# An adaLN block on one core: late modulation vectors as VectorE dot products, and a second full set of FFN weight buffers

## The chip, the cores and the metric

The kernel runs on one core of one Trainium2 chip. The metric is the device time of one execution in microseconds (us); the lower the better. Several executions are made of each kernel, and the median is given.

## The reference

The computation is one transformer block with adaptive layer norm. Six modulation vectors of 1024 values come from one row `c` by one product; everything else uses them.

```python
mod = (silu(c) @ w_mod).reshape(1, 6, 1, -1)        # w_mod: 1024 x 6144
sa, ca, ga, sb, cb, gb = (mod[:, i] for i in range(6))
h = layernorm(x) * (1 + ca) + sa                    # x: 2048 x 1024
q = h @ wq                                          # 1024 x 4096: 32 heads of 128
p = softmax(q @ k.T / sqrt(128))                    # the last 512 rows of the cache, 4 kv heads
x = x + ga * ((p @ v) @ wo)                         # wo: 4096 x 1024
h = layernorm(x) * (1 + cb) + sb
x = x + gb * ((silu(h @ w_gate) * (h @ w_up)) @ w_down)   # F = 3584
```

All inputs and the output are bf16.

## The kernel before

`fast_path` does the work; `general_path` stands behind a flag that `bound_final` (L983) computes, for scores too large for the plain exponential, and does not run here. TensorE's work is cut into four chunks (`cc`) of 512 rows.

**Startup.** Four tiles of x, the first two modulation vectors' weights (`wm`, L682), the weights of the first heads, K and V are loaded. The vectors `ca` and `sa` are computed as columns by TensorE, the first 512 rows are normalised and transposed, and the first three heads' q are made.

**The attention loop** (L1203 to L1215) has 128 steps, one head of one chunk each. Step k issues, in this order: a load of q weights in two of four steps, the scores and exponentials of head k (`emit_s`, L1025; the exponentials on ScalarE, L1034), the q projection of head k+3 (`emit_q`, L1015), then the tasks registered for step k, then the output product of head k-1 (`emit_o`, L1054). A task is a function and its arguments, registered with `at(step, function, ...)` (L806), and the tasks of one step run in the order in which they were registered. From step 13 on nearly every step has one `emit_wo` (L1090): eight matmuls of the output projection into one PSUM bank (`a_ps`), which VectorE then copies or adds into `acc` (L1102, L1104). Other tasks are loads of x and `wo`, transposes of the attention output by DMA (`xpose_o`, L1081), the layer norm of the next chunk and of the FFN's chunks (`plan_ln`), and the products `bound_wq` (L951, L955), 32 multiplications of weights with themselves on VectorE that feed the flag; four of them stand at step 32.

**The order.** In the attention loop DMAs and the statistics and bound products are pinned to the order in which the program issues them (`pin`, `fetch`); the scheduler of the framework places the rest by its own estimate. In the FFN the pins are off, and the scheduler decides the order of loads as well. Nearly all loads are issued by SP (SyncE), one after the other.

**Buffers.** Pools of equal buffers are handed out in turn, and a new tile waits until the old one in its buffer has been used: `hT` has 4 (8 KB per partition each), `blkA` 8, `blkB` 7, `blkC` 12. In PSUM four banks (tag "mm") are shared in turn by `q_ps`, `a_ps`, `o_ps` (three slots of a head's output in one bank) and `row_ps`; two pairs of banks hold scores, later the FFN's `gu_ps`. V lies in a tile of its own, `v_sb`, which is read last by the last output product of the attention loop.

**The late modulation vectors.** `ga` and `gb` (vectors 2 and 5) are needed as rows spread over all partitions (`ga_bc`, `gb_bc`, read at L1108 and L1192), `cb` and `sb` (4 and 3) as columns (`cb1`, `sb` in `modT`, read in the second layer norm at L856). They are computed during the first 33 steps in two pairs, (2, 4) and (5, 3). `load_rows` (L769) loads 1 MB of `w_mod` into a buffer of the `hT` pool. `mod_rows` (L774) runs 16 matmuls (L779) in which silu(c), repeated 32 times (`sil32`), is the weight and 512 columns of `w_mod` stream; four such products lie side by side in one bank. It runs in steps 5, 13, 21 and 29. VectorE copies the first half of the sum (L784) and adds the second (L788); the result goes to DRAM (`row_d`), and from there `load_gate` (L793) reads it back into all partitions and `load_cols` (L797) into columns, at steps 15 and 16 and again at 31 and 32. For `cb` VectorE then adds 1 (L802).

**The FFN loop** (L1217 ff.) goes over chunks; each has seven groups (`fg`) of four f-tiles. `load_gu` (L1154) loads a group's gate and up weights as four tiles of 512 KB, two of `wg` and two of `wu`, from the pool `blkB` of seven buffers. `emit_gu` (L1161) does eight matmuls with gate and eight with up weights for each f-tile (L1168); as long as tasks of the attention loop are left over (the last output projections among them), they run between the f-tiles. Then `emit_down` (L1181) multiplies with `w_down`.

Of the kernel before, what the change touches and what calls it, by code (L numbers as in the profile page):

```python
# [9 lines left out]
ALU = mybir.AluOpType  # L10
AX = mybir.AxisListType
BF16 = mybir.dt.bfloat16
FP32 = mybir.dt.float32
# [575 lines left out]
def fast_path(ctx, tc, flag, A_x, A_k_cache, A_v_cache, A_wq, A_wo, B_x, B_w_gate, B_w_up,  # L589
# [3 lines left out]
    nc = tc.nc  # L593
    P = 128
    _, S, D = A_x.shape
    _, Hkv, Sk, Dh = A_k_cache.shape
# [6 lines left out]
    TCW = 512  # L603
    NTC = S // TCW
    QT = TCW // P
    DT = D // P
# [5 lines left out]
    NFG = FT // 4  # L612
# [11 lines left out]
    wm_v = w_mod.rearrange("(dt p) n -> p dt n", p=P)  # L624
# [4 lines left out]
    const = ctx.enter_context(tc.tile_pool(name="const", bufs=1))  # L629
    xpool = ctx.enter_context(tc.tile_pool(name="xres", bufs=1))  # L630
    hpool = ctx.enter_context(tc.tile_pool(name="hT", bufs=4))
# [3 lines left out]
    wk = ctx.enter_context(tc.tile_pool(name="work", bufs=2))  # L635
    sm = ctx.enter_context(tc.tile_pool(name="small", bufs=4))
    psp = ctx.enter_context(tc.tile_pool(name="psum", bufs=4, space=bass.MemoryType.PSUM))
    dp = ctx.enter_context(tc.tile_pool(name="dram", bufs=4, space=bass.MemoryType.DRAM))
# [4 lines left out]
    def blkB(name, shape, dt=BF16):  # L643
        return pb_.tile(shape, dt, name=name, tag="B")

    def blkC(name, shape, dt=BF16):
        return pc_.tile(shape, dt, name=name, tag="C")

    def mm(name, shape=(P, 512), dt=FP32):
        return psp.tile(list(shape), dt, name=name, tag="mm", bufs=4)  # L650
# [9 lines left out]
    def pin(ins, what="steps"):  # L660
        return tc.keep_in_program_order(ins) if stage[what] else ins

    def fetch(out, in_):
        pin(nc.sync.dma_start(out=out, in_=in_), "dma")  # L664

    def load(out, in_):
        with nc.allow_non_contiguous_dma(reason="weight slice"):
            fetch(out=out, in_=in_)
# [33 lines left out]
    for kv in range(Hkv):  # L702
        pin(nc.sync.dma_start_transpose(
            out=kT[:, kv, :], in_=A_k_cache[0, kv, k0:k0 + W, :]), "dma")
    VN = Dh + 2
    v_sb = const.tile([P, Hkv, WT, Dh + 32], BF16, name="v_sb")
# [8 lines left out]
    ones_bf = const.tile([P, P], BF16, name="ones_bf")  # L715
# [15 lines left out]
    sa, ca1, sb, cb1 = (modT[:, i, :] for i in range(4))  # L731
    ga_bc = const.tile([P, D], FP32, name="ga_bc")
    gb_bc = const.tile([P, D], FP32, name="gb_bc")
# [7 lines left out]
    sil_r = const.tile([DT, P], BF16, name="sil_r")  # L741
# [3 lines left out]
    siluc = const.tile([P, DT], BF16, name="siluc")  # L745
# [12 lines left out]

    sil32 = const.tile([P, DT, 32], BF16, name="sil32")
    for dt in range(DT):
        nc.vector.tensor_scalar(out=sil32[:, dt, :], in0=ones_bf[:, 0:32],
                                scalar1=siluc[:, dt:dt + 1], scalar2=None, op0=ALU.mult)
    wm_rows = []
    row_part = []
    row_d = {}

    def load_rows(vec, part):  # L769
        t = hpool.tile([P, 4, D], BF16, name="wmr", tag="hT")  # L770
        load(t, wm_v[:, 4 * part:4 * part + 4, vec * D:(vec + 1) * D])
        wm_rows.append(t)

    def mod_rows(n, part):  # L774
        ps = mm("row_ps")
        tiles = [wm_rows.pop(0) for _ in range(2)]
        for k in range(4):
            for i in range(4):
                nc.tensor.matmul(ps[32 * i:32 * i + 32, :], lhsT=sil32[:, 4 * part + k, :],  # L779
                                 rhs=tiles[i // 2][:, k, (i % 2) * 512:(i % 2 + 1) * 512],  # L780
                                 start=(k == 0), stop=(k == 3))
        if part == 0:
            r = blkC("row", [P, TCW], FP32)
            nc.vector.tensor_copy(out=r, in_=ps)  # L784
            row_part.append(r)
        else:
            r = row_part.pop()
            nc.vector.tensor_tensor(out=r, in0=ps, in1=r, op=ALU.add)  # L788
            d = dp.tile([4, TCW], FP32, name="row_d", tag="row_d", bufs=2)
            fetch(out=d, in_=r[0:P:32, :])  # L790
            row_d[n] = d

    def load_gate(n, k, dst):  # L793
        fetch(out=dst.rearrange("p (a b) -> p a b", a=2),
                          in_=row_d[n][k:k + 2, :].partition_broadcast(P))

    def load_cols(n, k, dst, add_one):  # L797
        src = row_d[n][k:k + 2, :].rearrange("a (b p) -> p (a b)", p=P)
        with nc.allow_non_contiguous_dma(reason="1024 values to columns"):
            fetch(out=dst, in_=src)  # L800
        if add_one:
            nc.vector.tensor_scalar(out=dst, in0=dst, scalar1=1.0, scalar2=None, op0=ALU.add)  # L802

    tasks = {}

    def at(k, f, *a):  # L806
        tasks.setdefault(k, []).append((f, a))


    hT = {}  # L810
# [15 lines left out]
    def ln_norm(tt, on_act=False):  # L826
        mv = ln.pop(tt)
        n = wk.tile([P, D], BF16, name="xn", tag="xn", bufs=3)
        if on_act:
            nc.vector.scalar_tensor_tensor(out=mv[:, 3:4], in0=mv[:, 0:1], scalar=-1.0,  # L830
                                           in1=mv[:, 2:3], op0=ALU.mult, op1=ALU.mult)
            nc.scalar.activation(out=n, in_=xt[tt], func=ACT.Identity, bias=mv[:, 3:4],
                                 scale=mv[:, 2:3])
        else:
            pin(nc.vector.tensor_scalar(out=n, in0=xt[tt], scalar1=mv[:, 0:1],
                                        scalar2=mv[:, 2:3], op0=ALU.subtract, op1=ALU.mult))
        return n
# [85 lines left out]
    for t in range(QT):  # L923
        ln_stats(t)
        n = ln_norm(t, t % 2 == 0)
# [5 lines left out]
    for half in range(DH):  # L931
# [6 lines left out]
        for n in range(4 * LEAD):  # L938
            dt, g = (4 * half + n // LEAD, n % LEAD) if half == 0 else (4 + n % 4, n // 4)
            nc.tensor.matmul(q0_ps[g],  # L940
                             lhsT=wq_tiles[(0, 0, dt // 4)][:, dt % 4, g * P:(g + 1) * P],
                             rhs=hT[("h1", 0)][:, dt, :], start=(dt == 0), stop=(dt == DT - 1))
# [168 lines left out]
            nc.vector.tensor_tensor(out=x1, in0=f, in1=x1, op=ALU.add)  # L1111


    for n, vecs in enumerate(((2, 4), (5, 3))):
        for part in range(2):
            k = 16 * n + 8 * part
            at(k, load_rows, vecs[0], part)
            at(k + 2, load_rows, vecs[1], part)
            at(k + 5, mod_rows, n, part)
        at(16 * n + 15, load_gate, n, 0, gb_bc if n else ga_bc)  # L1120
        at(16 * n + 16, load_cols, n, 2, sb if n else cb1, n == 0)
    for tt in range(QT, S // P):
        cc, t = divmod(tt, QT)
        at(max((cc - 1) * H - 16, 0) + 2 + 2 * t, load_x, tt)
# [26 lines left out]
    gu_w = {}  # L1151
    wd_tiles = {}

    def load_gu(cc, fg):  # L1154
        for nm, v in (("wg", wg_v), ("wu", wu_v)):
            for i in range(2):
                t = blkB(nm, [P, 4, 512])
                load(t, v[:, 4 * i:4 * i + 4, fg * 512:(fg + 1) * 512])
                gu_w[(cc, fg, nm, i)] = t

# [113 lines left out]
```

## Time and profile before

| | |
|---|---|
| median of 11 executions | 1285.49 us (1284.01 to 1288.64) |
| the profiled execution | 1284.41 us |
| its span in the profile | 1282.6 us |
| TensorE busy, granted clock | 1262.2 us (98%), 0.998 |
| VectorE busy | 577.6 us (45%) |
| ScalarE busy | 333.9 us (26%) |
| GpSimd busy | 1.2 us |
| moved by DMA | 204.21 MB, 159 GB/s on average |

The span runs from the first to the last instruction that the profile shows; the execution's own time is 1.8 us longer. A page of the profile lists for each group of equal instructions the engine, the operation, the tiles that it writes and reads, the count, the busy time, the mean of one and the engine's idle time just before it with what ended that. The list of waits gives, for one engine, the instruction that waited, for which other one, the total, the count and the longest. PE is TensorE, DVE VectorE, ACT ScalarE, SPq the queue of SyncE, whose entries last as long as the issue of the transfer takes. The transfer's landing comes later. "x16" after a matmul in a timeline means that sixteen like it follow without a gap and are shown as one piece.

### The profile page before, as it was taken

What the parts mean: (1) busy time and instruction counts of PE and PEld (TensorE: products, weight loads), DVE (VectorE), ACT (ScalarE), POOL (GpSimd) and SP (SyncE); (2) the same over time, 40 slices, a digit from 0 to 9 for tenths busy, and PEclk for the clock granted to TensorE, in tenths of its full rate; (3) what the DMA queues carried; (4) which work ended last, traced back from release to release, by engine and by line L of the source; (5) the groups of instructions that cost most, each with busy time, mean ns of one, the idle gap of its engine ahead of it and who ended that gap; (6) DMA issues with size and microseconds to landing.
All of it is one profiled execution on the core that took longest, in us unless ns stands there. A gap on an engine that the chain in (4) does not pass through costs nothing.

```text
span 1282.6 us, 17999 instructions
## 1 busy us (share of the span) xinstructions
PE 1262.2 (98%) x7461; PEld 642.5 (50%) x7601; DVE 577.6 (45%) x1271; ACT 333.9 (26%) x433; POOL 1.2 (0%) x8
## 2 busy tenths in 40 slices
PE   8999999999999999999999999999999999999998
PEld 4555555555555555555554444444444444444444
DVE  4464467865577756576653642221212221221122
ACT  3543334333333433333341111011100111011100
POOL 0000000000000000000000000000000000000000
PEclk9999999999999999999999999999999999999999
DMA  9988466557345654445587484454536455464401
GB/s 291 271 208 227 154 152 170 140 147 197 92 128 156 144 146 142 120 145 131 132 204 223 141 236 148 140 189 146 179 103 219 141 164 164 136 193 133 146 21 48
DMA packets 280111, 204.21 MB, mean 159 GB/s; under 512 B 113868, under 2 KB 273612, under 8 KB 280021
## 3 DMA queue, kind: packets, MB, share of 16 engines
q1 hardware_dynamic: 275106, 198.78, 54.2%
q10 hardware_dynamic: 4912, 4.20, 1.0%
q8 instruction: 61, 1.00, 0.3%
q14 instruction: 32, 0.24, 0.1%
HBM read 174.08 MB, written 4.21 MB: 139 GB/s over the span
## 4 chain that ended last, share of the span: by engine, by line
PE 95%; DMA 2%; DVE 1%; SPq 1%; issue 1%; ACT 0%; DVEq 0%
PE gu_ps L1168 29%; PE a_ps L1096 17%; PE q_ps L1019 16%; PE d_ps L1188 15%; PE o_ps L1064 9%; PE s_ps L1032 8%; DMA wm<-in_w_mod_dram 1%; SPq L664 1%; DMA modT<-row_d 0%; DMA hT<-xn 0%; DMA wu<-in_B_w_up_dram 0%; PE row_ps L779 0%; PE q_ps L940 0%; DMA oT<-oq 0%; DVE st L816 0%
## 5 line engine op out<-in xcount | busy, mean ns | idle before, releaser
L1034 ACT ACTIVATE pT<-s_ps 128x1024 bf16<-128x1024 f32 x256 | 248.7, 1020 | 341.8 <-PE s_ps L1032 228.4
L1096 PE MATMUL a_ps<-wo,oT 128*128 128x512 bf16 x986 | 239.9, 379 | 3.0 <-DVE acc L1102 1.0
L1019 PE MATMUL q_ps<-hT,wq 128*128 128x512 bf16 x999 | 236.7, 379 | 0.3 <-DVE modT L755 0.3
L1168 PE MATMUL gu_ps<-hT,wu 128*128 128x512 bf16 x875 | 209.9, 379 | 3.0 <-DMA wu<-in_B_w_up_dram 1.8
L1168 PE MATMUL gu_ps<-hT,wg 128*128 128x512 bf16 x879 | 210.0, 379 | 0.9
L1174 DVE TENSOR_TENSOR guT<-gu_ps,sg 128x512 bf16<-128x512 f32 x112 | 77.4, 691 | 283.6 <-ACT sg L1173 283.6
L1173 ACT ACTIVATE sg<-gu_ps 128x512 bf16<-128x512 f32 x112 | 66.9, 597 | 490.7 <-PE gu_ps L1168 376.7
L1188 PE MATMUL d_ps<-wd,guT 128*128 128x512 bf16 (+2 forms) x935 | 193.3, 366 | 0.9
L916 DVE CAST qT<-q_ps 128x512 bf16<-128x512 f32 x128 | 88.3, 691 | 176.7 <-PE q_ps L1019 176.2
L1096 PEld LDWEIGHTS <-oT 128*128 128x128 bf16 x1024 | 99.9, 98 | 122.3 <-issue 2.1
L1019 PEld LDWEIGHTS <-wq 128*128 128x128 bf16 x1000 | 97.8, 98 | 117.8 <-issue 0.3
L1188 PEld LDWEIGHTS <-guT 128*128 128x128 bf16 x952 | 90.9, 98 | 103.0
L1064 PEld LDWEIGHTS <-pT 128*128 128x128 bf16 x2048 | 126.6, 98 | 30.6 <-issue 0.4
L1168 PEld LDWEIGHTS <-wu 128*128 128x128 bf16 x896 | 87.6, 98 | 107.8 <-DMA wu<-in_B_w_up_dram 2.3
L1168 PEld LDWEIGHTS <-wg 128*128 128x128 bf16 x896 | 87.6, 98 | 105.5
L1064 PE MATMUL o_ps<-v_sb,pT 128*128 128x130 bf16 x2048 | 137.1, 220 | 0.0
L1032 PE MATMUL s_ps<-qT,kT 128*128 128x512 bf16 x467 | 129.2, 379 | 2.9 <-ACT pT L1034 0.6
L1051 DVE TENSOR_TENSOR oq<-o_ps,rl 128x256 bf16<-128x256 f32 (+2 forms) x256 | 101.2, 419 | 4.3
L1192 DVE TENSOR_TENSOR f<-d_ps,gb_bc 128x512 f32<-128x512 f32 (+2 forms) x34 | 22.4, 660 | 147.1 <-PE d_ps L1188 133.2
L1104 DVE TENSOR_TENSOR acc<-a_ps,acc 128x512 f32<-128x512 f32 x64 | 44.0, 688 | 38.3 <-PE a_ps L1096 38.3
L1032 PEld LDWEIGHTS <-kT 128*128 128x128 bf16 x512 | 44.9, 98 | 31.7 <-issue 1.3
L816 DVE BATCH_NORM_STATS2 st<-x 128x6 f32<-128x512 bf16 x64 | 41.3, 680 | 2.8 <-DMA x<-in_A_x_dram 2.5
(75 smaller groups left out, 308.5 us busy)
## 6 DMA issues: line engine op xcount, KB each, us to landing
wq<-in_A_wq_dram SPq DMA_DIRECT2D x64, 512.0 KB, 4.2
wo<-in_A_wo_dram SPq DMA_DIRECT2D x64, 512.0 KB, 5.8
wg<-in_B_w_gate_dram SPq DMA_DIRECT2D x56, 512.0 KB, 5.5
wu<-in_B_w_up_dram SPq DMA_DIRECT2D x56, 512.0 KB, 3.8
wd<-in_B_w_down_dram SPq DMA_DIRECT2D x56, 512.0 KB, 6.5
wmr<-in_w_mod_dram SPq DMA_DIRECT2D x8, 1024.0 KB, 11.3
x<-in_A_x_dram SPq DMA_DIRECT2D x16, 256.0 KB, 5.8
wm<-in_w_mod_dram SPq DMA_DIRECT2D x4, 1024.0 KB, 10.2
```

The lines of the kernel that those rows point to most:

```text
L916: nc.vector.tensor_copy(out=t, in_=q_ps)
L1019: nc.tensor.matmul(q_ps, lhsT=wq_tiles[(cc, h // 4, dt // 4)][:, dt % 4, (h % 4) * P:(h % 4 + 1) * P], rhs=hT[("h1", cc)][:, dt, :], start ...
L1032: nc.tensor.matmul(s_ps[:, i, :], lhsT=kT[:, kv, j * P:(j + 1) * P], rhs=qT[g], start=True, stop=True)
L1034: nc.scalar.activation(out=p[:, 2 * jj:2 * jj + 2, :], in_=s_ps, func=ACT.Exp, scale=scale)
L1051: nc.vector.tensor_tensor(out=dst, in0=ps[:, s0:s0 + cnt, 0:Dh], in1=sc, op=ALU.mult)
L1064: nc.tensor.matmul(o_slot["ps"][:, s_, :], lhsT=pT[g][:, j, t * P:(t + 1) * P], rhs=v_sb[:, kv, j, 0:VN], start=(j == 0), stop=(j == WT - 1))
L1096: nc.tensor.matmul(a_ps, lhsT=oT[(cc, 2 * q + i)][:, hh % 4, t * P:(t + 1) * P], rhs=wo_tiles[(cc, q, dh, i)][:, hh % 4, :], start=(hh == ...
L1104: nc.vector.tensor_tensor(out=acc[(cc, t)][:, dsl], in0=a_ps, in1=acc[(cc, t)][:, dsl], op=ALU.add)
L1168: nc.tensor.matmul(ps[:, n, :], lhsT=gu_w[(cc, fg, nm, dt // 4)][:, dt % 4, fi * P:(fi + 1) * P], rhs=hT[("h2", cc)][:, dt, :], start=(dt ...
L1173: nc.scalar.activation(out=g, in_=ps[:, 0, :], func=ACT.Silu)
L1174: nc.vector.tensor_tensor(out=guT[(cc, fg)][:, fi, :], in0=ps[:, 1, :], in1=g, op=ALU.mult)
L1188: nc.tensor.matmul(d_ps, lhsT=guT[(cc, f // 4)][:, f % 4, t * P:(t + 1) * P], rhs=wd_tiles[(cc, dh, f // 4)][:, f % 4, c0:c0 + w], start=( ...
```

## The change

Two edits. The first, in `load_gu`: in every group whose number `cc * 7 + fg` is odd, the second `wu` tile is not taken from `blkB` but lies where V was (`v_blk`, a view of `v_sb`'s first 2048 elements per partition), so that eight places take turns for four tiles of a group.

The second replaces the row products of the late modulation vectors. `spread_c` at step 0 writes silu(c) to DRAM and reads it back into all 128 partitions (`c_bc`). `load_wmT` loads 128 columns of `w_mod` (1024 rows of 256 bytes, 12,288 bytes apart; 256 KB) with a transposing DMA, so that each column lies in one partition; four share one buffer of the `hT` pool. There are 32 of them, one in nearly every second step from 1 to 67. `mod_dot`, three steps after each, multiplies such a tile with `c_bc` on VectorE and adds the products up along the row (`accum_out`), which gives 128 values of the vector as one column; the order on VectorE is pinned. The vectors come in the order 2, 4, 3, 5: dots stand in steps 4 to 18, 20 to 34, 36 to 50 and 54 to 70. `cb` gets its 1 added at step 35. The gates, which are wanted as rows, are transposed by VectorE, stored by four small DMAs (steps 19 and 71) and read back into all partitions (steps 22 and 74). GpSimd clears two small tiles at the start.

```diff
--- before.py
+++ after.py
@@ -758,48 +758,47 @@
 
 
 
-    sil32 = const.tile([P, DT, 32], BF16, name="sil32")
-    for dt in range(DT):
-        nc.vector.tensor_scalar(out=sil32[:, dt, :], in0=ones_bf[:, 0:32],
-                                scalar1=siluc[:, dt:dt + 1], scalar2=None, op0=ALU.mult)
-    wm_rows = []
-    row_part = []
-    row_d = {}
-
-    def load_rows(vec, part):
-        t = hpool.tile([P, 4, D], BF16, name="wmr", tag="hT")
-        load(t, wm_v[:, 4 * part:4 * part + 4, vec * D:(vec + 1) * D])
-        wm_rows.append(t)
-
-    def mod_rows(n, part):
-        ps = mm("row_ps")
-        tiles = [wm_rows.pop(0) for _ in range(2)]
-        for k in range(4):
-            for i in range(4):
-                nc.tensor.matmul(ps[32 * i:32 * i + 32, :], lhsT=sil32[:, 4 * part + k, :],
-                                 rhs=tiles[i // 2][:, k, (i % 2) * 512:(i % 2 + 1) * 512],
-                                 start=(k == 0), stop=(k == 3))
-        if part == 0:
-            r = blkC("row", [P, TCW], FP32)
-            nc.vector.tensor_copy(out=r, in_=ps)
-            row_part.append(r)
-        else:
-            r = row_part.pop()
-            nc.vector.tensor_tensor(out=r, in0=ps, in1=r, op=ALU.add)
-            d = dp.tile([4, TCW], FP32, name="row_d", tag="row_d", bufs=2)
-            fetch(out=d, in_=r[0:P:32, :])
-            row_d[n] = d
-
-    def load_gate(n, k, dst):
-        fetch(out=dst.rearrange("p (a b) -> p a b", a=2),
-                          in_=row_d[n][k:k + 2, :].partition_broadcast(P))
-
-    def load_cols(n, k, dst, add_one):
-        src = row_d[n][k:k + 2, :].rearrange("a (b p) -> p (a b)", p=P)
-        with nc.allow_non_contiguous_dma(reason="1024 values to columns"):
-            fetch(out=dst, in_=src)
-        if add_one:
-            nc.vector.tensor_scalar(out=dst, in0=dst, scalar1=1.0, scalar2=None, op0=ALU.add)
+
+
+    c_d = dp.tile([DT, P], BF16, name="c_d", tag="c_d", bufs=1)
+    c_bc = const.tile([P, D], BF16, name="c_bc")
+    gcol = [const.tile([P, 32], FP32, name=f"gcol{n}") for n in range(2)]
+    grow = const.tile([P, 32], FP32, name="grow")
+    for n in range(2):
+        nc.gpsimd.memset(gcol[n], 0.0)
+    wm_cols = {}
+    col_d = {}
+
+    def spread_c():
+        fetch(out=c_d, in_=sil_r)
+        fetch(out=c_bc.rearrange("p (a b) -> p a b", a=DT), in_=c_d.partition_broadcast(P))
+
+    def load_wmT(vec, j):
+        if j % 4 == 0:
+            wm_cols[(vec, j // 4)] = hpool.tile([P, 4, D], BF16, name="wmT", tag="hT")
+        c0 = vec * D + j * P
+        pin(nc.sync.dma_start_transpose(out=wm_cols[(vec, j // 4)][:, j % 4, :],
+                                        in_=w_mod[:, c0:c0 + P]), "dma")
+
+    def mod_dot(vec, j, dst):
+        t = wm_cols[(vec, j // 4)]
+        junk = wk.tile([P, D], BF16, name="junk", tag="junk", bufs=1)
+        pin(nc.vector.scalar_tensor_tensor(out=junk, in0=t[:, j % 4, :], scalar=1.0, in1=c_bc,
+                                           op0=ALU.mult, op1=ALU.mult,
+                                           accum_out=dst[:, j:j + 1]))
+
+    def add_one(dst):
+        pin(nc.vector.tensor_scalar(out=dst, in0=dst, scalar1=1.0, scalar2=None, op0=ALU.add))
+
+    def store_gate(n):
+        d = dp.tile([DT, P], FP32, name="col_d", tag="col_d", bufs=2)
+        pin(nc.vector.transpose(out=grow, in_=gcol[n]))
+        for q in range(4):
+            fetch(out=d[:, 32 * q:32 * q + 32], in_=grow[32 * q:32 * q + DT, :])
+        col_d[n] = d
+
+    def load_gate(n, dst):
+        fetch(out=dst.rearrange("p (a b) -> p a b", a=DT), in_=col_d[n].partition_broadcast(P))
 
     tasks = {}
 
@@ -1111,14 +1110,19 @@
             nc.vector.tensor_tensor(out=x1, in0=f, in1=x1, op=ALU.add)
 
 
-    for n, vecs in enumerate(((2, 4), (5, 3))):
+    at(0, spread_c)
+    for vec, dst, starts in ((2, gcol[0], (1, 9)), (4, cb1, (17, 25)), (3, sb, (33, 41)),
+                             (5, gcol[1], (51, 61))):
         for part in range(2):
-            k = 16 * n + 8 * part
-            at(k, load_rows, vecs[0], part)
-            at(k + 2, load_rows, vecs[1], part)
-            at(k + 5, mod_rows, n, part)
-        at(16 * n + 15, load_gate, n, 0, gb_bc if n else ga_bc)
-        at(16 * n + 16, load_cols, n, 2, sb if n else cb1, n == 0)
+            for i in range(4):
+                at(starts[part] + 2 * i, load_wmT, vec, 4 * part + i)
+                at(starts[part] + 2 * i + 3, mod_dot, vec, 4 * part + i, dst)
+        k = starts[1] + 10
+        if vec == 4:
+            at(k, add_one, cb1)
+        elif vec in (2, 5):
+            at(k, store_gate, vec // 5)
+            at(k + 3, load_gate, vec // 5, gb_bc if vec == 5 else ga_bc)
     for tt in range(QT, S // P):
         cc, t = divmod(tt, QT)
         at(max((cc - 1) * H - 16, 0) + 2 + 2 * t, load_x, tt)
@@ -1151,10 +1155,15 @@
     gu_w = {}
     wd_tiles = {}
 
+    v_flat = v_sb.rearrange("p a b c -> p (a b c)")
+    v_blk = v_flat[:, 0:2048].rearrange("p (a b) -> p a b", a=4)
+
     def load_gu(cc, fg):
+
         for nm, v in (("wg", wg_v), ("wu", wu_v)):
             for i in range(2):
-                t = blkB(nm, [P, 4, 512])
+                spare = (cc * NFG + fg) % 2 == 1 and nm == "wu" and i == 1
+                t = v_blk if spare else blkB(nm, [P, 4, 512])
                 load(t, v[:, 4 * i:4 * i + 4, fg * 512:(fg + 1) * 512])
                 gu_w[(cc, fg, nm, i)] = t
 
```

## The prediction

> **What bounds the kernel now.** I read the page first, then the list of waits of TensorE, then the chain of work in order of time, and went from each gap to the timeline around it.
>
> ```profile
> span 1282.6 us, 17999 instructions
> PE 1262.2 (98%) x7461; PEld 642.5 (50%) x7601; DVE 577.6 (45%) x1271; ACT 333.9 (26%) x433; POOL 1.2 (0%) x8
> ...
> DVE  4464467865577756576653642221212221221122
> ```
>
> TensorE is busy 98% of the span at an undisturbed clock (mean 0.998). So time is won only by taking matmuls away or by closing one of its few gaps; VectorE (45%) is loaded unevenly, most in slices 4 to 19 (32 us each), which are the attention loop.
>
> ```profile
> PE mod_ps L753 <- DMA wm<-in_w_mod_dram: 1.9, 2, 1.3
> PE gu_ps L1168 <- DMA wu<-in_B_w_up_dram: 1.8, 1, 1.8
> ...
> PE a_ps L1096 <- DVE acc L1102: 1.0, 1, 1.0
> ```
>
> These are TensorE's longest waits (total, times, longest); the line left out and the first belong to the startup, the other two are inside the change's reach. The chain in order of time names the transfers behind those two (start, duration):
>
> ```profile
> 85.63 5.08 DMA modT<-row_d
> ...
> 750.46 4.24 DMA wu<-in_B_w_up_dram
> ```
>
> **What the Trainium skill says.** "TensorEngine Tiling (Array Packing)", section Key Properties, says that different tiles of the array work in parallel. The trace agrees: in the second row group 16 matmuls of 128\*32 with a recorded 379 ns each fill only 1.05 us. So the row matmuls are priced by that group, not by their busy sum. "Perfetto Trace Analysis", section Matmuls, wants matmul groups rotated through PSUM banks, so that evacuation overlaps the next group. The attention loop does that with four banks, and the slack this leaves decides what extra VectorE work costs. "DMA: Bandwidth & Descriptors", section Latency and other measured facts, gives transposing DMAs 261 GB/s with a strided source: an estimate of 1.0 us of transfer for 256 KB. No row here has that source; the nearest, `hT<-xn`, moves 256 KB and lands in 3.2 us at the median.
>
> **Part 1: 64 row matmuls go.** Groups of 16 ran in steps 5, 13, 21 and 29.
>
> ```profile
> L779 PE MATMUL row_ps<-wmr,sil 128*32 128x512 bf16 x64 | 4.2, 382 | 0.0
> ```
>
> From the starts of the score matmuls, step 13 takes 77.94 - 71.64 = 6.30 us, and the step after it 83.17 - 77.94 = 5.23. The four steps are longer by 1.08 on average: 4.35 us, all on TensorE and all on the path. Gain 4.35. With them go 8 small VectorE operations for `sil32`, four of 0.69 us on `row`, and 8 loads of 1 MB. These lie beside TensorE's work: nothing more.
>
> **Part 2: the column load's wait goes.** In the first column load VectorE waits at L802 for a DMA, with the evacuation of an `a_ps` bank queued behind it:
>
> ```profile
> 90.73 0.17 DVE L802 TENSOR_SCALAR modT<-modT 128x8 f32<-128x8 f32 x1 [3.62 <-DMA modT<-row_d]
> ...
> 91.42 0.67 DVE L1102 COPY acc<-a_ps 128x512 f32<-128x512 f32 x1
> ```
>
> Of the 3.6 us the free banks cover the larger part. Steps 15 and 16 together take 11.60 us where two regular steps take 2 x 5.22 = 10.44: 1.16 lost. After the change the addition (step 35) reads what VectorE itself wrote. The late gate loads are waited for by nobody before L1108 and L1192. Gain 1.16.
>
> **Part 3: VectorE gets 32 dot products.** The bound products at L955 are the same operation in form and size: 32 of them take 1.216 us each on average and 0.083 for the accumulator's read, so 1.30 per dot, 32 x 1.30 = 41.6 us, between steps 4 and 70. TensorE loses only where a bank is given back late. A regular step ends with banks free 1.9 to 2.4 us before their next use (end of the evacuation to first matmul). One dot sits behind the `qT` copy and ahead of the `a_ps` evacuation and delays that by 1.3; then VectorE's idle time in the rest of the pair of steps repays it. I carried the lag from step to step, with that step's idle time as repayment. In steps 36 to 46, where layer-norm statistics and affine passes share VectorE, the lag peaks near 1.8 us against about 2.4; in 64 to 70 it peaks lower, since the dot there goes ahead of a bound product that now comes after the evacuation. No stall. One place has no slack: step 32, with four bound products at once.
>
> ```profile
> 178.08 0.69 DVE L916 CAST qT<-q_ps 128x512 bf16<-128x512 f32 x1 [2.04 <-PE q_ps L1019]
> 178.68 1.22 DVE L955 SCALAR_TENSOR_TENSOR junk<-wq 128x1024 bf16<-128x1024 bf16 x1
> ...
> 184.59 0.67 DVE L916 CAST qT<-q_ps 128x512 bf16<-128x512 f32 x1
> ```
>
> VectorE does not rest from 178.08 to 186.1, and the banks come free only 0.05 (`o_ps`) and 0.19 us (`q_ps`) ahead. A dot of 1.3 to 1.5 us added there, less those 0.05 to 0.2, and less the 0.65 us by which three score matmuls now go ahead of the blocked ones, is 0.5 to 1.3. I take 0.9. Bounds: 0 if the order hides it, 2.0 if step 34 pays again.
>
> **Part 4: what SP issues.** 32 transposes replace 8 loads of 1 MB, with the same 8 MB read; twelve small DMAs (two for c, eight stores, two gates) replace six. An issue takes 1.25 us (`hT`) to 2.9 (the kT transposes' longest); two in four steps are 2.5 to 5.8 us on top of some 10 us of issue, in 20.9. That fits, since SP stands waiting for VectorE hundreds of us in total. Landing: `hT` 3.2 at the median, `kT` (half the size, same kind of source) 6.0 at the median and 8.5 at most; bounds 3.2 to 17 (twice the longest `kT`), taken 5. Issue to dot is three steps: 15.7 us, some 14 after the issue, 9 for the first, which also stands behind c_d, which must land before c_bc is issued. The skill, same DMA page, section Two DMAs through the same engine are not ordered, says why that wait is needed. The DMA engines' busy share between 26 and 42 us was 1.03; it sinks, since 1 MB then replaces 4. Cost 0, with L (landing) below 14.
>
> **Part 5: the FFN weights.** One stall is the whole of FFN's waiting for weights:
>
> ```profile
> 743.77 6.59 SPq L848 DMA_TRANSPOSE hT<-xn  x4
> 750.46 0.53 SPq L664 DMA_DIRECT2D wu<-in_B_w_up_dram  x1
> ...
> 751.88 1.03 PE L1168 MATMUL gu_ps<-hT,wu 128*128 128x512 bf16 x4
> 754.75 1.04 PE L1168 MATMUL gu_ps<-hT,wu 128*128 128x512 bf16 x4 [1.85 <-DMA wu<-in_B_w_up_dram]
> ```
>
> With seven buffers the eighth tile waits for an old one and lands in the queue behind four `hT` transposes. Matmuls of x4 should go on at 752.75 and start at 754.75: 2.0 lost. With two full sets each tile goes where a tile of two groups before lay, which has been free for a whole group (64 matmuls at 0.216 us, from 8 in 1.73, are 13.8 us) when the new one is due; in SP's order after the change this tile stands ahead of the four transposes. V itself is read last at about 673, before the odd groups ask for its place. Next late would be the gate tiles of the group after, which stand behind the transposes as before: issued at 751.1, by the page 5.5 us to landing, due 13.8 us after this group's start at 750.15, so over 6 us to spare. Gain 2.0; bounds 0 and 2.0.
>
> **Sum.** 4.35 + 1.16 + 2.0 - 0.9 = 6.6. The profiled execution took 1284.41, of which the span is 1282.6; so span 1276.0, execution 1277.8. The median, 1285.49, is 1.08 above it: 1278.9, rounded to 1279.0. About 0.2% (2.6 us) is what a measurement can tell from none: faster is below 1282.9, slower above 1288.1.
>
> **Rivals.**
> VectorE becomes the bound in places: if a dot costs 0.3 us in about ten of the 32 (steps 36 to 46, 64 to 70), 3 us come back, with 0.2 to 0.6 us each 2 to 6: 1281 to 1285. For: smallest remaining slack by my count is 0.5 us. Against: VectorE idles 0.2 to 1.6 in every step.
> The FFN stall moves: the queue after the change holds eight loads at once and another one is 2 us late: 1281.0. For: DMA share 1.09 around it. Against: due times a group later.
> Slower: a transposed tile lands so late that VectorE waits in front of the evacuation at each dot. Source rows of 256 B at a pitch of 12 KB have no row here. A landing beyond 14 + 1.5 us (the bank slack) stalls TensorE at each of 28 steady dots; it decides from 0.35 us more, 28 x 0.35 = 9.8 us, so at L = 15.9; at 16.5 it is 28 us: 1307. For: the upper bound of 17. Against: the same bytes in `hT` land in 3.2.
> That nothing changes is excluded for part 1: 64 matmuls are gone.
>
> **How the numbers follow.** As summed (1277 to 1281.5): 58%, all faster. VectorE rival (1281 to 1285, seldom above): 16%, of it 7 faster, 8 same, 1 slower. FFN rival (1279 to 1283.5): 13%, 9 faster, 4 same. Slower rival: 10%. Better than summed (below 1276.5, the 0.9 not paid and more): 3%. Faster 77, same 12, slower 11. The range 1276.0 to 1286.0 leaves out about 14%.
>
> **What would show it.** Right: no `row_ps` and no `modT<-row_d` in the waits; the wu wait gone; regular steps still 5.22 with dots in them; a gap of about 0.9 around step 32. Wrong: TensorE waiting for `acc`, `qT` or o evacuations in steps 36 to 46; VectorE waiting at a dot for `wmT`; a new weight wait in the FFN.

## The result and the profile after

The changed kernel takes 1276.81 us (median of 8 executions, 1276.32 to 1277.8), the kernel before, run again beside it, 1286.09 us. The ratio is 0.9928 (95% interval 0.9918 to 0.9937): 9.3 us less, by the interval 8.1 to 10.5. The forecast was 1279.0 in a range of 1276.0 to 1286.0, and 6.6 us less.

| | before | after |
|---|---|---|
| the profiled execution | 1284.41 us | 1275.46 us |
| its span | 1282.6 us | 1273.7 us |
| TensorE busy | 1262.2 us | 1255.7 us |
| VectorE busy | 577.6 us | 606.5 us |
| start of the weight load of the first score matmul | 26.12 us | 24.44 us |

Lines of code after the change are one less than before in the attention loop (L955 is L954), and nine more in the FFN (L1168 is L1177). First the head of the page after the change, then TensorE's longest waits (total, times, longest).

```profile
span 1273.7 us, 17958 instructions
PE 1255.7 (99%) x7396; PEld 640.5 (50%) x7537; DVE 606.5 (48%) x1325; ACT 333.7 (26%) x433; POOL 1.3 (0%) x10
...
DVE  4575578867587755576663641221122112221122
```

```profile
PE warm_ps L727 <- POOL warm_w L721: 1.5, 1, 1.5
PE h_ps L926 <- ACT xn L831: 1.1, 2, 0.8
PE q_ps L939 <- ACT hT L852: 1.1, 1, 1.1
```

No wait for `wu` or for `acc` is left, as forecast. But the wait for `wm` in the startup, which the forecast left where it was, has gone too. What is left of the longer waits is the startup's own.

The gains lie at few places. Each score matmul of before has its counterpart after; the difference between their starts was followed along the kernel, and where it changes by more than 0.2 us, that place gained or lost:

| place | change of the start, us |
|---|---|
| before the first scores | -1.68 |
| steps 5, 13, 21 and 29 (row matmuls gone) | -1.08 each, -4.33 in all |
| steps 15 and 16 (wait at L802 gone) | -1.16 |
| steps 33 and 34 | -0.23, then +0.53: +0.30 |
| FFN, the stall for `wu` | -2.02 |
| sum | -8.89 |

Everywhere else, with the 32 dots running, the difference changes by no more than 0.12 us from one step to the next. The sum is the difference of the spans (8.9). Steps 13 and 14 show it after the change: both take 5.2 us, where step 13 took 6.30 before. And the matmuls with `wu`, which stood still for 1.85 us before, follow one another.

```profile
68.87 1.03 PE L1031 MATMUL s_ps<-qT,kT 128*128 128x512 bf16 x4
...
74.10 1.03 PE L1031 MATMUL s_ps<-qT,kT 128*128 128x512 bf16 x3
...
79.32 1.03 PE L1031 MATMUL s_ps<-qT,kT 128*128 128x512 bf16 x4
...
745.01 1.89 PE L1177 MATMUL gu_ps<-hT,wu 128*128 128x512 bf16 x8
746.74 1.89 PE L1177 MATMUL gu_ps<-hT,wg 128*128 128x512 bf16 x8
```

Where VectorE was to be loaded most, the timeline after the change shows the same close packing as before, one dot earlier (start, duration; the last lines are TensorE's):

```profile
170.91 0.69 DVE L915 CAST qT<-q_ps 128x512 bf16<-128x512 f32 x1 [2.04 <-PE q_ps L1018]
171.52 1.22 DVE L786 SCALAR_TENSOR_TENSOR junk<-wmT,c_bc 128x1024 bf16<-128x1024 bf16 x1
...
178.57 0.67 DVE L915 CAST qT<-q_ps 128x512 bf16<-128x512 f32 x1
...
181.66 0.69 DVE L915 CAST qT<-q_ps 128x512 bf16<-128x512 f32 x1 [0.81 <-PE q_ps L1018]
```

```profile
177.66 0.84 PE L1063 MATMUL o_ps<-v_sb,pT 128*128 128x130 bf16 x12
178.34 0.81 PE L1031 MATMUL s_ps<-qT,kT 128*128 128x512 bf16 x3
179.29 0.39 PE L1063 MATMUL o_ps<-v_sb,pT 128*128 128x130 bf16 x4
```

From 170.91 to the copy at 178.57 VectorE does not rest, and the first copy that finds it idle again is that at 181.66. On TensorE three score matmuls stand ahead of the output matmuls whose bank VectorE still holds, so the backlog costs little, and once.

### The profile page after: what moved, and what is told of

It is laid out like the page before. It is cut to its first block, busy times and chain, and to the rows that moved or that the text cites. A ratio compares the mean times of both kernels' runs of the same rounds, so it can differ in the third digit from the quotient of the medians.

```text
span 1273.7 us, 17958 instructions
## 1 busy us (share of the span) xinstructions
PE 1255.7 (99%) x7396; PEld 640.5 (50%) x7537; DVE 606.5 (48%) x1325; ACT 333.7 (26%) x433; POOL 1.3 (0%) x10
## 4 chain that ended last, share of the span: by engine, by line
PE 97%; DVE 1%; issue 1%; ACT 0%; DMA 0%
PE gu_ps L1177 30%; PE a_ps L1095 17%; PE q_ps L1018 17%; PE d_ps L1197 15%; PE o_ps L1063 9%; PE s_ps L1031 8%; PE q_ps L939 0%; DVE junk L954 0%; DVE st L815 0%; DMA x<-in_A_x_dram 0%; PE mod_ps L753 0%; ACT pT L1033 0%; DVE qT L915 0%; ACT xn L831 0%; PE h_ps L926 0%
## 5 line engine op out<-in xcount | busy, mean ns | idle before, releaser
L1177 PE MATMUL gu_ps<-hT,wg 128*128 128x512 bf16 x875 | 209.8, 379 | 1.0
L1177 PE MATMUL gu_ps<-hT,wu 128*128 128x512 bf16 x659 | 162.0, 379 | 0.7
L1177 PEld LDWEIGHTS <-wg 128*128 128x128 bf16 x896 | 87.6, 98 | 105.5
L1177 PEld LDWEIGHTS <-wu 128*128 128x128 bf16 x672 | 65.8, 98 | 79.3
L1177 PE MATMUL gu_ps<-hT,v_sb 128*128 128x512 bf16 x220 | 57.0, 379 | 0.2
```

The lines of the kernel that those rows point to most:

```text
L1177: nc.tensor.matmul(ps[:, n, :], lhsT=gu_w[(cc, fg, nm, dt // 4)][:, dt % 4, fi * P:(fi + 1) * P], rhs=hT[("h2", cc)][:, dt, :], start=(dt ...
```

## The experiments

Each was timed against runs of the kernel before on the same chip; the ratios are to these.

**The FFN buffer alone.** The kernel before with the edit of `load_gu`.

```diff
-                t = blkB(nm, [P, 4, 512])
+                spare = (cc * NFG + fg) % 2 == 1 and nm == "wu" and i == 1
+                t = v_blk if spare else blkB(nm, [P, 4, 512])
```

> The kernel before with the FFN buffer edit alone; the late modulation vectors stay row matmuls. My theory: the one weight stall at 752.8 us goes and nothing else moves, 2.0 us faster than the kernel before (ratio 0.9984), no TensorE wait for wu left. Rival (the stall moves to another tile because eight loads are on the way at once): another weight wait of about 2 us appears and the time is that of the kernel before.

1284.49 us, ratio 0.9988 (0.9982 to 0.9995): 1.3 us less by the medians, 0.6 to 2.3 by the interval. The wait for `wu` is gone, and 1.70 us are gained there. But the next f-tile loses 1.19 again, so 0.5 of it is left at this place in the profiled execution:

```profile
PE mod_ps L753 <- DMA wm<-in_w_mod_dram: 1.4, 1, 1.4
PE gu_ps L1172 <- DVE guT L1178: 1.2, 2, 1.0
PE a_ps L1096 <- DVE acc L1102: 1.1, 1, 1.1
```

VectorE waits there 2.66 us for the four `hT` transposes, and the product `guT`, which gives TensorE its bank back, is queued behind that. So the stall did move in this kernel, though not to another weight. In the changed kernel the same wait is 2.34 us and TensorE loses nothing. The four transposes took 7.30 us to issue in this run and 6.03 in the changed kernel. That asks for a difference between the kernels' transfers. One is found below; it turns out to be only a part of the answer here.

**The dots alone.** The changed kernel with all FFN tiles in `blkB` again.

```diff
-                t = v_blk if spare else blkB(nm, [P, 4, 512])
+                t = blkB(nm, [P, 4, 512])
```

> The changed kernel with the FFN buffer edit undone; dot products stay. My theory: the changed kernel plus 2.0 us, thus 1278.8 (ratio to before 0.9944), with the wu wait of the kernel before back. Rival (the two parts share a gain, because the dots alone already move the FFN loads): under 0.5 us slower than the changed kernel.

1277.9 us, ratio 0.9934 (0.9920 to 0.9949): 1.1 us more than the changed kernel by the medians, though the intervals overlap. The wait for `wu` is back, with 0.55 us in the timeline instead of 1.85, and the FFN gains 1.30 against before without any edit there. So the rival was partly right: something that came with the dots made these loads faster.

```profile
748.37 1.04 PE L1177 MATMUL gu_ps<-hT,wu 128*128 128x512 bf16 x4 [0.55 <-DMA wu<-in_B_w_up_dram]
```

**Two tries at the startup.** In the startup the change takes away one thing that can be seen, eight VectorE operations for `sil32` (1.18 us) ahead of the third and fourth tile's statistics; with them gone the scheduler puts two groups of transposes ahead of 32 `mod_ps` matmuls. One kernel puts them back into the changed kernel, unread; one moves them to step 2 in the kernel before.

```diff
+    sil32 = wk.tile([P, DT, 128], BF16, name="sil32", tag="junk", bufs=1)
+    for dt in range(DT):
+        nc.vector.tensor_scalar(out=sil32[:, dt, 0:32], in0=ones_bf[:, 0:32],
+                                scalar1=siluc[:, dt:dt + 1], scalar2=None, op0=ALU.mult)
```

> The changed kernel with the eight small VectorE operations of sil32 put back at the start, unread. In the trace the first scores begin 1.68 us earlier after the change than before, which the prediction did not have. Theory S: these eight operations (1.18 us) delay the third and fourth normalised tile, and the scheduler then puts 32 mod_ps matmuls that wait for a late wm load ahead of the transposes on TensorE; with them back the start is late again: first scores 1.1 to 1.7 us later, 1278.0 to 1278.5 in all. Rival D (the wm loads merely landed later in the profiled execution of before, by chance): no change, 1276.8, first scores at 24.4 as in the changed kernel, or scattered without regard to sil32.

1276.27 us, ratio 0.9920 (0.9906 to 0.9934): no loss.

```diff
-    for dt in range(DT):
-        nc.vector.tensor_scalar(out=sil32[:, dt, :], in0=ones_bf[:, 0:32],
-                                scalar1=siluc[:, dt:dt + 1], scalar2=None, op0=ALU.mult)
+
+    def spread_sil():
+        for dt in range(DT):
+            pin(nc.vector.tensor_scalar(out=sil32[:, dt, :], in0=ones_bf[:, 0:32],
+                                        scalar1=siluc[:, dt:dt + 1], scalar2=None,
+                                        op0=ALU.mult))
...
+    at(2, spread_sil)
```

> The kernel before with the eight operations of sil32 moved from the startup to step 2 of the attention loop; all else as before. Theory S: the order of TensorE's startup becomes that of the changed kernel, first scores near 24.4 instead of 26.1, and the time 1.2 to 1.7 us less than before (ratio 0.9987 to 0.9991). Rival D: same as the kernel before, 1286.1.

1286.4 us, ratio 1.0001 (0.9992 to 1.0010): no gain. The order of TensorE's startup became that of the changed kernel, and yet its scores did not begin earlier (27.7 us, a part of it the clock, see the end): TensorE now met the last `wm` load earlier and waited for it 1.53 us:

```profile
18.73 0.87 PE L753 MATMUL mod_ps<-siluc,wm 128*128 128x1 bf16 x29
21.13 0.95 PE L753 MATMUL mod_ps<-siluc,wm 128*128 128x1 bf16 x32 [1.53 <-DMA wm<-in_w_mod_dram]
```

Theory S, the operations of `sil32`, has fallen. What bounds this startup is when the loads land. And here the runs fell into two sets: between 10 and 15 us the kernel before, the FFN buffer alone and this one took in 348 to 350 GB/s, the changed kernel and the two made from it 386, though SyncE issues the same transfers in the same order up to 24 us. Rival D, chance, does not fit these two sets.

**The layout.** What differs is where the tiles lie. Pools come after the constants in SBUF; `sil32` has gone and `c_bc`, `gcol` and `grow` have come, 1920 bytes more in sum. The pools' tiles begin 128 bytes past a multiple of 512 before, and at a multiple of 512 after. Padding undoes that either way without moving one instruction in the order of any engine.

```diff
-    sil32 = const.tile([P, DT, 32], BF16, name="sil32")
+    sil32 = const.tile([P, DT, 56], BF16, name="sil32")
```

> The kernel before with 384 more bytes per partition in the tile of sil32, unused; every engine's order of instructions is the same. Theory S has fallen. Theory L (layout): in the kernel before all the pools' tiles begin 128 bytes past a multiple of 512 in SBUF, in the changed kernel at a multiple of 512, because c_bc and the small tiles are 1920 bytes larger in sum than sil32; in the first 20 us packets of 1024 bytes then took 51.5 ns before and 46.1 after, and 350 against 386 GB/s came in. Theory L expects here 46 ns and 386 GB/s between 10 and 15 us, the last wm load in time (no wait at 21.2 us), a shorter wu wait in the FFN (about 0.6 instead of 1.9), and 1.5 to 2.7 us less than the kernel before (ratio 0.9979 to 0.9988). Rival (the faster loads come from the other transfers of the changed kernel, not from the layout): 51 ns, 350 GB/s, and the time of the kernel before.

1283.38 us, ratio 0.9981 (0.9971 to 0.9990): 2.7 us less than the kernel before, for nothing but a wider tile. For the other direction `grow` in the changed kernel is made 128 bytes wider.

```diff
-    grow = const.tile([P, 32], FP32, name="grow")
+    grow = const.tile([P, 64], FP32, name="grow")
```

> The changed kernel with 128 more bytes per partition in a small tile, unused, so that the pools' tiles begin 128 bytes past a multiple of 512 as in the kernel before; the order of instructions is the same. Theory L expects 51 ns and 350 GB/s between 10 and 15 us, a wait for wm of about 1.5 us in the startup, and 1.3 to 2.5 us more than the changed kernel: 1278.1 to 1279.3. Rival: no change, 1276.8.

1278.09 us, ratio 0.9934 (0.9920 to 0.9947): 1.3 us more than the changed kernel by the medians; the intervals overlap. The wait for `wm` is back, and a wait for `guT` of 0.5:

```profile
PE mod_ps L753 <- DMA wm<-in_w_mod_dram: 1.9, 2, 1.7
...
PE gu_ps L1177 <- DVE guT L1183: 0.5, 1, 0.5
```

The windows from 10 to 14 us tell the layouts apart whatever else the kernel holds. The last number is GB/s, the one before it the busy share of the DMA engines. Before, after, padded by 384, and after the change off by 128, in this order:

```profile
10.00:14.00 4.00, 2.65 (x78) 2.33 (x76) 1.94 (x13) 2.12 (x5) 0.00 (x0) 1.00 1.10 348
```

```profile
10.00:14.00 4.00, 3.63 (x70) 2.68 (x69) 1.30 (x5) 1.92 (x5) 0.00 (x0) 1.00 1.09 386
```

```profile
10.00:14.00 4.00, 2.82 (x80) 2.50 (x79) 2.11 (x14) 2.12 (x5) 0.00 (x0) 1.00 1.09 385
```

```profile
10.00:14.00 4.00, 3.63 (x69) 2.68 (x68) 1.31 (x5) 1.93 (x5) 0.00 (x0) 1.00 1.10 349
```

The busy share is the same, the bytes are not: between 10 and 15 us a packet of 1024 bytes takes 51.6 ns on average in the first case and 46.0 in the second. The last kernel of this set asks which multiple matters.

```diff
-    sil32 = const.tile([P, DT, 32], BF16, name="sil32")
+    sil32 = const.tile([P, DT, 40], BF16, name="sil32")
```

> The kernel before with 128 more bytes per partition, so that the pools' tiles begin 256 bytes past a multiple of 512. If only a multiple of 512 is fast (theory L as stated), it is as the kernel before: 51 ns, 350 GB/s. If a multiple of 256 is enough, it is as the run with 384 bytes. The rival to the layout expects no difference to the kernel before either way, in both padded runs.

1283.86 us, ratio 0.9980 (0.9973 to 0.9988); 46.0 ns and 385 GB/s. So 256 is enough, and "a multiple of 512" was too narrow. Its profiled execution still has a wait of 1.9 us for `wu`, so not every stall in the FFN follows the layout: the stall for `wu` became 0.78 us shorter in the kernel padded by 384, and no shorter in this one.

**The wait at L802 alone.** In the kernel before the addition to `cb1` goes to step 20.

```diff
-        at(16 * n + 16, load_cols, n, 2, sb if n else cb1, n == 0)
+        at(16 * n + 16, load_cols, n, 2, sb if n else cb1)
+    at(20, add_one, cb1)
```

> The kernel before with one edit: the addition of 1 to cb1 is issued four steps later (step 20) than the load of the columns, so that VectorE need not wait for that DMA. My theory: the 1.16 us at steps 15 and 16 go and nothing else, a_ps waits for acc no more: 1.2 us less than before (ratio 0.9991). Rival (the bank wait comes from VectorE's load in these steps, not from the DMA): a wait of about 1 us stays.

1284.35 us, ratio 0.9986 (0.9980 to 0.9993). In the trace the scores of step 17 come 1.16 us earlier relative to the steps before, and TensorE no longer waits for `acc`. VectorE waits for TensorE at the copy that was held up before, and no more for a DMA. The theory holds.

```profile
88.76 0.69 DVE L1103 COPY acc<-a_ps 128x512 f32<-128x512 f32 x1 [0.58 <-PE a_ps L1097]
```

**The loss at step 33.** The bound products of step 32 are spread over steps 29 to 32.

```diff
-                at((1 + hg % (NTC - 1)) * H + max(0, 4 * hg - 3 + 2 * i + j), bound_wq, hg, i, j)
+                at((1 + hg % (NTC - 1)) * H + 4 * hg - 3 + 2 * i + j, bound_wq, hg, i, j)
```

> The changed kernel with the four bound products of step 32 spread over steps 29 to 32, as those of the other head groups are. In the changed kernel the scores of step 34 come 0.23 us earlier and those of step 35 0.53 later against before: 0.30 lost in all, where the prediction had 0.9. My theory: the loss comes from VectorE's backlog of four bound products and a dot; spread, it is gone, steps 32 to 35 take 5.22 us each, and the time is 0.3 us less than that of the changed kernel (1276.5), which only the profile can show. Rival (the loss belongs to the new order of matmuls at step 33 whatever VectorE does): 0.3 stays.

1277.26 us, ratio 0.9929 (0.9916 to 0.9943), which can't be told from the changed kernel. In the trace the 0.30 are gained back (+0.23, -0.53 against the changed kernel), and steps 32 to 35 start 5.22 us apart. So the loss was VectorE's backlog. That this arrangement is better is shown by its trace alone, not by its time.

**How much room VectorE had.** Each dot twice, with the same result in the same place.

```diff
-        pin(nc.vector.scalar_tensor_tensor(out=junk, in0=t[:, j % 4, :], scalar=1.0, in1=c_bc,
-                                           op0=ALU.mult, op1=ALU.mult,
-                                           accum_out=dst[:, j:j + 1]))
+        for _ in range(2):
+            pin(nc.vector.scalar_tensor_tensor(out=junk, in0=t[:, j % 4, :], scalar=1.0, in1=c_bc,
+                                               op0=ALU.mult, op1=ALU.mult,
+                                               accum_out=dst[:, j:j + 1]))
```

> The changed kernel with each of the 32 dot products issued twice in a row (the second overwrites the first with the same values): 41.6 us more on VectorE between steps 4 and 70. By the bookkeeping of the prediction (lag up to 1.8 of 2.4 us with one dot, idle 0.2 to 1.6 us in a step) a second dot doesn't fit in steps 36 to 46: TensorE then waits for banks there, 5 to 15 us more than the changed kernel. Rival (VectorE's room was much larger than counted): under 1 us more.

1278.11 us, ratio 0.9936 (0.9921 to 0.9951). VectorE's dots take twice as long:

```profile
L787 DVE SCALAR_TENSOR_TENSOR junk<-wmT,c_bc 128x1024 bf16<-128x1024 bf16 x64 | 77.8, 1216 | 0.0
...
L787 DVE DVE_READ_ACCUMULATOR junk<-wmT,c_bc 128x1 f32 x64 | 5.3, 83 | 0.0
```

The scores fall behind those of the changed kernel by 1.49 us between step 0 and step 47, all of it at step 35 and steps 44 to 47: 0.75 and 0.74. My 5 to 15 were far too many, though the places were right; the rival's "under 1 us" was closer in spirit and a little low.

**How late a tile may land.** The dots one step after their loads.

```diff
-                at(starts[part] + 2 * i + 3, mod_dot, vec, 4 * part + i, dst)
+                at(starts[part] + 2 * i + 1, mod_dot, vec, 4 * part + i, dst)
```

> The changed kernel with each dot product one step after its transposing load instead of three, 10.4 us less between them (7 in the first steps). In the changed kernel's trace the dots start 10 to 29 us after the end of the load's issue, and a load's 1024 packets of 256 bytes are through about 3.3 us after the issue begins. My theory (landing near 3.5 us): all dots but a few of the first still come late enough; VectorE waits for wmT a few times, under 2 us each, TensorE loses less than 1 us. The slower rival of the prediction (landing of 8 us and more) would make VectorE wait at most dots and cost over 20 us.

1276.33 us, ratio 0.9922 (0.9907 to 0.9937): no loss at all. All transposing loads, all dots, and the empty list of what they waited for:

```profile
L780 SPq DMA_TRANSPOSE wmT<-in_w_mod_dram x32: 1160/1223/2990, 30.2 to 349.4; - x32
L786 DVE SCALAR_TENSOR_TENSOR junk<-wmT,c_bc x32: 1212/1216/1218, 35.8 to 361.9; 128x1024 bf16<-128x1024 bf16 x32
...
its engine sat idle before it (us, times) until:
who waited for it (us, times):
```

The shortest time from the end of an issue to its dot is 2.43 us here, and VectorE did not wait. Had landings taken 8 us and more after the issue, as in the slower rival, the dots that came sooner would have waited; so that is excluded.

**All but the dots.** The kernel before with V's place as a buffer, 384 bytes of padding and the addition at step 20: the three edits shown above, together.

> The kernel before with the three other gains put in and the row matmuls kept: V's place as a buffer, 384 bytes of padding, the addition to cb1 at step 20. What is left between it and the changed kernel is the four groups of row matmuls (4.32) less the loss at step 33 (0.30). If my sum closes, it takes 1276.8 + 4.0 = 1280.8 us, the median ratio to before 0.9960, no wait for wu, acc or guT of 0.5 us or more on TensorE, and steps 5, 13, 21 and 29 stay 1.08 us longer. Rival (the gains overlap, or something unnamed belongs to the dots): off by more than 1.5 us.

1281.58 us, ratio 0.9961 (0.9949 to 0.9974). The ratio is what the sum asked for (0.9960); the medians are 4.8 us apart where the sum had 4.0, within the interval. Between this kernel and the changed one steps 5, 13, 21 and 29 differ by 1.08 us each, and steps 33 and 34 give 0.30 back. Against the expectation one wait for `guT` of 0.7 us stays in the FFN, at the f-tile where the buffer alone lost 1.19; TensorE loses 0.82 there, and nothing in the changed kernel.

```profile
PE gu_ps L1174 <- DVE guT L1180: 0.7, 1, 0.7
```

## Why the prediction was right, and what it left out

**Row matmuls: right.** 4.33 us against 4.35. The price came from the difference of whole steps, not from the group's busy sum (4.2) or from 64 times 379 ns; each of the four steps gave 1.08.

**The wait at L802: right.** 1.16 against 1.16, and it goes alone when it is taken away alone.

**The dots on VectorE: right that regular steps don't stall, mis-sized in the rest.** One dot cost 1.30 us of VectorE, as the bound product's row said. No step from 4 to 70 but one pair shows it on TensorE. The term "0.9 at step 32" measured 0.30: of the backlog the reordered score matmuls and the free banks covered more than was counted (no run separates the two). The "smallest remaining slack of 0.5 us" was far too cautious. A second dot of 1.30 everywhere cost 1.5 us in all. The bookkeeping let a step's lag go on into the next with only that step's visible idle time as repayment; a likely reason is that it counted VectorE's idle time in front of a `qT` copy as lost, while a late copy has room of its own, since q is made three steps ahead. That reason wasn't tried by itself.

**SyncE and landing: right in the result, the margin mis-sized to the safe side.** The issue of a transpose took 1.22 us at the median (taken 1.25 to 2.9). The dots stood 10 to 30 us after the end of their issue, where the forecast had 9 for the first and some 14 for the rest: SyncE runs ahead of the steps. With 2.43 us it was still enough. Of the 1.0 us of transfer for 256 KB, which the prediction estimated from the Trainium skill's "DMA: Bandwidth & Descriptors", section Latency and other measured facts, no run here tells more than that the whole landing fits in 2.43 us and the issue.

**The FFN: 2.02 against 2.0, and the closeness is in part luck.** That the buffer ends the stall for `wu` was right. What the prediction left out is the wait that comes next: it looked for it at the gate tiles, but it was VectorE's, for the four `hT` transposes, with `guT` behind it. Alone the buffer gave 0.5 us at that place in its trace and 1.3 by the medians; and the dots alone had gained 1.30 of the same stall without the buffer. Four kernels with the buffer show what was lost at the f-tile after the stall, and how long SyncE took to issue the four transposes, in one profiled execution each:

| with the buffer | lost, us | four transposes, us |
|---|---|---|
| row matmuls, tiles off by 128 (buffer alone) | 1.19 | 7.30 |
| row matmuls, tiles aligned (all but the dots) | 0.82 | 7.00 |
| dots, tiles off by 128 | 0.65 | 6.33 |
| dots, tiles aligned (the changed kernel) | 0 | 6.03 |

Four more kernels with dots and aligned tiles lose nothing there either, at 5.3 to 5.8 us for the transposes. So in these executions the full 2.0 came only with both, the layout and the dots in place of the row matmuls. Why the dots make these transposes quicker stays open.

**What was left out.** The forecast of 6.6 us was 2.7 short of the measured 9.3. The named steps gave 7.2 us (4.33 + 1.16 + 2.02 - 0.30), 0.6 more than forecast, because the loss at step 33 was smaller. The rest is for the most part a term that the prediction put at nothing: the layout of SBUF. It was worth 2.7 and 2.2 us when the kernel before was given an aligned layout, and 1.3 by the medians, with overlapping intervals, when the changed one lost it. It has no instruction of its own, so no order of instructions shows it; it is in the addresses. It can't be added to the 7.2 in full, since a part of the FFN's 2.02 is the layout's too: 0.65 of it was lost when the changed kernel went off by 128. Without that part the named steps are 6.6, and with 1.3 to 2.7 for the layout the sum is 7.9 to 9.3, beside a measured interval of 8.1 to 10.5. It closes within the uncertainty of these medians and no closer.

A part of the layout's gain can be seen in the startup. There the last `wm` load lands at 21.1 to 21.3 us in the three kernels off by 128 in which TensorE waited for it, and at 19.6 to 20.1 in the four aligned ones in which it did. The granted clock disturbs a comparison of first scores (see below), so only executions are compared in which it dips from 20 us on: in the two off by 128 the scores begin at 27.7 and 27.9 us, in the five aligned ones at 26.2 to 26.7. That is 1.0 to 1.7 us. In the executions with an earlier dip the two layouts don't separate (26.1 to 27.2 against 25.6 and 27.4). So the 1.68 us at the startup of the two profiles are not all layout.

In the median of before there is a shift of 0.6 us too: it was 1285.49 in the 11 executions that the forecast started from and 1286.09 in all.

## What to carry to other kernels

Price a removed group by the length of the steps with and without it, and test each wait that goes for what is queued behind it: the row matmuls and the wait at L802 came out within 0.03 us that way, and the FFN's stall, tested for the wrong next wait, did not when it was removed alone. When an edit changes the size of any tile, compare the addresses of all the tiles that transfers write to, as well as the order of instructions; and when two kernels load the same bytes in the same order at different rates, look there first. Spare bytes that bring the tiles to a multiple of 256 cost nothing and gave 2.2 and 2.7 us here.

## What the runs showed of the hardware

**Alignment of a transfer's destination.** With tiles 128 bytes past a multiple of 256 the loads between 10 and 15 us came in at 348 to 350 GB/s (five kernels), with tiles on a multiple of 256 at 385 to 386 (nine kernels, multiples of 512 in eight, 256 in one). A packet of 1024 bytes took 51.6 ns there before the change and 46.0 after it. The Trainium skill's page "DMA: Bandwidth & Descriptors", section How a descriptor splits into AXI transactions, says that a descriptor that doesn't start at a multiple of 256 bytes begins with a transaction at the boundary below, whose unused bytes still cost beats of 32. For 1024 bytes from 128 on an estimate by that rule is 36 beats instead of 32, 12.5% more; the packets between 10 and 15 us show 12%. The page speaks of reads; here it is the writing side, in SBUF, that was moved. And the rest of the traces shows that the beats are not the price of every packet: between 600 and 1200 us, in most of it the FFN, the median packet of 1024 bytes takes 46 ns in all 14 kernels, and only the means differ, 50.3 to 51.1 ns off by 128 and 49.0 to 49.9 aligned. Why the full 12% appears in the startup alone is not shown.

**A short dip of the granted clock in the startup.** In 12 of the 14 profiled executions TensorE's granted clock falls to 0.5 for 3.4 us (nine executions) or 6.8 us (three) somewhere between 12 and 28 us; in the changed kernel's and in that of the kernel padded by 384 it doesn't. The profile of before has it too, though its mean of 0.998 made the prediction call the clock undisturbed (the number before the last two is the clock):

```profile
14.00:16.00 2.00, 1.78 (x16) 1.35 (x15) 0.49 (x2) 0.40 (x1) 0.00 (x0) 0.54 1.10 349
16.00:18.00 2.00, 2.00 (x7) 0.71 (x6) 0.74 (x2) 1.16 (x2) 0.00 (x0) 0.60 1.10 352
```

Of the aligned kernels' executions the two without a dip began their first scores at 24.4 and 24.6 us, the seven with one at 25.6 to 27.4. After the first scores the changed kernel, the one with `sil32` put back and the one with early dots run alike to 0.01 us up to the FFN's last gate and up weights, so the startup is where such executions differ. The changed kernel's profiled execution, 1275.46, is 1.35 us below its own median, and a difference of 1 to 2 us at the start of two profiles shows nothing by itself. What brings the dip stays open.

**A transposing load** of 1024 rows of 256 bytes, 12,288 bytes apart, cost SyncE 1.22 us to issue at the median, and the one with the least time before its dot was in place within 2.43 us of the issue's end.
